# Two of three attention units by rows until unit 121, and LayerNorm statistics a slot earlier

## The chip, the cores and the metric

The kernel runs on one NeuronCore of a Trainium2 chip. Its engines are TensorE (PE, with its weight loads shown as PEld), VectorE (DVE), ScalarE (ACT), GpSimd (POOL) and SyncE (SP), which issues nearly all DMAs. Each engine works through its own queue in order and waits on semaphores of the others. The metric is the device time of one execution in microseconds, as the median of several runs.

## The reference

One block of a conditioned transformer: an attention with cached keys and values, then a gated MLP with a spatial mixing matrix, each behind a LayerNorm that is modulated by a condition vector `c`.

```python
mod = (_silu(c) @ w_mod).reshape(c.shape[0], 6, 1, -1)      # sa, ca, ga, sb, cb, gb
h = _layernorm(x) * (1 + ca) + sa
# A: q = h @ wq (32 heads of 128), 8 groups of cached k, v; softmax(q k / sqrt(128)) v @ wo
x = x + ga * _A_ref(h, A_k_cache, A_v_cache, A_wq, A_wo)
h = _layernorm(x) * (1 + cb) + sb
# B: z = gelu(h @ w_in); z1, z2 = halves; z2 = _layernorm(z2); g = w_sp @ z2 + b_sp; (z1 * g) @ w_out
x = x + gb * _B_ref(h, B_w_in, B_w_sp, B_b_sp, B_w_out)
```

There are 2048 tokens of 512 features in bfloat16, 2048 cached keys, 8 groups of 4 heads that share keys and values, and 896 features in each half of the MLP.

## The kernel before

**Units and passes.** Attention is cut into 128 units: 8 groups times 16 tiles of 128 tokens. Unit u belongs to group u // 16 and tile j = u % 16, and covers the 4 heads of its group. The main loop has one pass `it` for each unit and six more at its end; pass `it` makes the scores of unit `it`, the PV sum (probabilities times values) of earlier units, and the output projection of still earlier ones. A pass has 8 slots. The order inside a slot is fixed by the program: first what `at(it, slot, fn)` has put down for it (the list `later`, in the order of registration), then the scores `qk`, then PV, then a piece of the next block's q projection (`fill`), then a matmul of the output projection, which takes the last slots of a pass. The schedule is manual, so each engine's queue keeps the program's order.

**Two forms of a unit.** A *column unit* computes the scores transposed (L1029), keys on the partitions; ScalarE's exponential writes them straight into `pTs[u]`. PV then takes 64 matmuls of 129 columns (`pv`, L1085), the last column being the row sum; DVE divides (L1096, L1097: `onorm`), SP turns the result by a DMA transpose into `oT` (L1108), and the output projection sums 4 matmuls in one PSUM bank, which DVE adds to `xacc` once (L1129). A *row unit* computes the scores with queries on the partitions (L1010); the exponential (L1017) writes rows into one of six row buffers `pn` and leaves sums, SP transposes each head's rows into `pTs[u]` (`turn_rows`, L1049), and DVE makes the reciprocal of the sums (L1053, L1056). PV takes 16 matmuls of 512 columns (`pv_rows`, L1064) and DVE copies them to `oT` (L1073). Each head's projection matmul then has a bank of its own, which DVE scales and adds to `xacc` (L1135, four times). The `pn` buffers lie where `win_sb`, the MLP's first weight, is loaded later (L1276).

`by_rows(u)` says which form a unit has: from TURN_A = 8 up to TURN_B, two of every three. `LAGS` gives a row unit's PV two or three passes after its scores; a column unit's comes one pass after.

```python
TURN_A, TURN_B = 2 * CT, NU - CT * 2 - 1     # 8 and 119; NU = 128, CT = 4
LAGS = (2, 3, 1)
def by_rows(u):
    return TURN_A <= u < TURN_B and (u - TURN_A) % len(LAGS) < len(LAGS) - 1
def pv_at(u):
    return u + (LAGS[(u - TURN_A) % len(LAGS)] if by_rows(u) else 1)
def wo_at(u):
    return pv_at(u) + (3 if u < NU - 6 else 2)
```

With this, passes 118, 119, 120, 121, 122, 123 hold the PV of units 116, 118, 117 and 119, 120, 121, 122, and passes 121 to 126 hold the output projections of 116; 118; 117 and 119; 120; 121 and 122; 123.

**Banks.** PSUM has two banks of scores (`s_ps`, each 1024 wide), two `o_ps` banks for PV and two `misc` banks, which the q projection (L946, cast to SBUF by DVE at L957) and the output projection (L1142) take in turn.

**The end of a tile.** When the last group's projection of tile j is complete, `xacc` times `ga_rows` plus x becomes the new `x_sb` tile: on POOL for tiles 0 to 11 (L1158, L1159), on DVE for 12 to 15. `ln2` then normalises it in three steps, put down for later slots: `first` takes the statistics on DVE (L697 bn_stats, L698) and the reciprocal root on POOL (L678, L682); `second` normalises on DVE (L686) and has SP transpose the result into `xnT2` (L1180; two buffers); `third` modulates it into the MLP's input `hT` on DVE (L1187, four instructions).

Of the kernel before, what the change touches and what calls it, by code (L numbers as in the profile page):

```python
# [575 lines left out]
def kernel(  # L576
# [28 lines left out]
    NT = S // P  # L605
# [4 lines left out]
    CT = 512 // P  # L610
# [64 lines left out]
    def rstd_of(mv, n, tag):  # L675

        ve = stat.tile([P, CT], FP32, name=f"ve_{tag}")
        nc.gpsimd.tensor_scalar(  # L678
            out=ve[:, :n], in0=mv[:, :, 1], scalar1=LN_EPS, scalar2=None, op0=ALU.add
        )  # L680
        rstd = stat.tile([P, CT], FP32, name=f"rstd_{tag}")
        nc.gpsimd.tensor_tensor(out=rstd[:, :n], in0=ve[:, :n], in1=mhalf[:, :n], op=ALU.pow)  # L682
        return rstd

    def normalise(dst, src, mv, rstd):
        nc.vector.tensor_scalar(  # L686
            out=dst,
            in0=src,
            scalar1=mv,
            scalar2=rstd,  # L690
            op0=ALU.subtract,
            op1=ALU.mult,
        )

    def ln_stats(mv, j, src):
        st = stat.tile([P, 1, nc.vector.BN_STATS_DIM], FP32, name="bnst")
        nc.vector.bn_stats(out=st[:, 0, :], in_=src)  # L697
        nc.vector.bn_aggr(out=mv[:, j, :], in_=st[:])  # L698
# [97 lines left out]
    def ln1_stats(j0, n):  # L796
        for j in range(j0, j0 + n):
            ln_stats(mv1, j, x_sb[:, j, :])
        return rstd_of(mv1[:, j0 : j0 + n, :], n, "ln1")
# [161 lines left out]
    first = dict(r1=ln1_stats(1, 1))  # L961


    NU = HKV * NT


    TURN_A, TURN_B = 2 * CT, NU - CT * 2 - 1

    LAGS = (2, 3, 1)

# [21 lines left out]
    def at(it, slot, fn):  # L992
        later.setdefault((it, slot), []).append(fn)
# [173 lines left out]
    def ln2(it, j):  # L1167

        st = {}

        def first():
            if j < NT - CT:
                ln_stats(mv2, j, x_sb[:, j, :])
            st["rstd"] = rstd_of(mv2[:, j : j + 1, :], 1, "ln2")

        def second():
            xn = res.tile([P, D], BF16, name="xn2", bufs=2)
            normalise(xn[:], x_sb[:, j, :], mv2[:, j, 0:1], st["rstd"][:, 0:1])
            st["xnT"] = res.tile([P, NDT, P], BF16, name="xnT2", bufs=2)
            nc.sync.dma_start_transpose(out=st["xnT"][:], in_=xn[:])  # L1180

        def third():
            ch, c0 = j // CT, (j % CT) * P
            if ch not in h2Ts:
                h2Ts[ch] = res.tile([P, NDT, 512], BF16, name="hT", bufs=NCH)
            for dt in range(NDT):
                nc.vector.tensor_scalar(  # L1187
                    out=h2Ts[ch][:, dt, c0 : c0 + P],
                    in0=st["xnT"][:, dt, :],
                    scalar1=modc[:, 4 * NDT + dt : 4 * NDT + dt + 1],  # L1190
                    scalar2=modc[:, 3 * NDT + dt : 3 * NDT + dt + 1],
                    op0=ALU.mult,
                    op1=ALU.add,
                )

        at(it + 1, 0 if j >= NT - CT else 3, first)
        at(it + 1, 4 if j >= NT - CT else 5, second)
        at(it + 2, 5, third)

    mod_b = {}  # L1200
# [109 lines left out]
    for g in range(1, HKV):  # L1310
        it = (g - 1) * NT
# [106 lines left out]
    for it in range(NU + 6):  # L1418
# [26 lines left out]
        for u in wos:  # L1445
            if u >= (HKV - 1) * NT:
                ln2(it, u % NT)
# [185 lines left out]
```

## Time and profile before

| | |
|---|---|
| median of 3 runs | 1308.66 us (1308.49 to 1308.84) |
| the profiled execution | 1308.74 us |
| its span, first to last instruction | 1306.8 us |
| PE busy | 1298.8 us, 99% of the span |
| ACT busy | 1113.5 us, 85% |
| DVE busy | 674.7 us, 52% |
| POOL busy | 56.6 us, 4% |
| granted TensorE clock | 1.000 |

The profile is of one execution. Busy is the time in which an engine ran at least one instruction; a matmul's end is modelled and matmuls overlap, so the spacing of starts tells more than durations. A timeline line has the start, the duration of what is merged in it, the engine, the source line and the operation with what it writes and reads; in square brackets stands how long the engine was idle before it, and what ended that. A wait line has who waited, for whom, the total, how often and the longest.

### The profile page before, as it was taken

The numbers are of one execution on the slowest core, as the hardware profiler recorded it, in microseconds if no ns is written. First come the engines' busy times: TensorE is split into PE (matmuls) and PEld (weight loads), VectorE is DVE, ScalarE is ACT, GpSimd is POOL, SyncE is SP. The second block draws the span as 40 slices with busy tenths as digits, with TensorE's granted clock in tenths as the row PEclk, the third lists the DMA queues.
The fourth block names the chain that finished last, engine by engine and source line by source line (L and its number), as shares of the span: only waits on it lengthen the run. The fifth ranks groups of instructions, "written<-read, shape, count | busy, mean of one in ns | idle before, by whom it ended". The sixth has DMA issues, their size and how long they took to land.

```text
span 1306.8 us, 22904 instructions
## 1 busy us (share of the span) xinstructions
PE 1298.8 (99%) x8809; PEld 705.7 (54%) x8809; DVE 674.7 (52%) x1740; ACT 1113.5 (85%) x1653; POOL 56.6 (4%) x92
## 2 busy tenths in 40 slices
PE   9999999999999999999999999999999999999998
PEld 5665555555555555555555555555555566644445
DVE  5534445544554455445544554455455657694443
ACT  7899999999999999999999999999999988650000
POOL 1000000000000000000000000000000134210000
PEclk9999999999999999999999999999999999999999
DMA  7469999999999999999999999999999921364300
GB/s 183 125 127 188 163 193 183 190 168 187 189 188 168 192 168 195 177 170 186 189 189 170 187 189 179 180 188 174 182 187 171 166 82 29 57 137 98 78 20 31
DMA packets 743878, 203.33 MB, mean 156 GB/s; under 512 B 728144, under 2 KB 742608, under 8 KB 743760
## 3 DMA queue, kind: packets, MB, share of 16 engines
q1 hardware_dynamic: 741168, 199.55, 83.1%
q10 hardware_dynamic: 2592, 2.23, 0.6%
q8 instruction: 71, 1.16, 0.4%
q14 instruction: 47, 0.39, 0.1%
HBM read 21.37 MB, written 2.10 MB: 18 GB/s over the span
## 4 chain that ended last, share of the span: by engine, by line
PE 92%; DVE 0%; issue 0%
PE o_ps L1064 20%; PE s_ps L1010 19%; PE o_ps L1085 13%; PE s_ps L1029 12%; PE misc L1142 8%; PE misc L946 8%; PE misc L1500 7%; PE s_ps L1335 2%; PE s_ps L1374 2%; PE o_ps L1533 1%; PE s_ps L1533 0%; PE o_ps L856 0%; DVE xacc L1135 0%; DVE tmp L1545 0%; DVE bnst L697 0%; DVE qT L957 0%
## 5 line engine op out<-in xcount | busy, mean ns | idle before, releaser
L1010 PE MATMUL s_ps<-kT,qT 128*128 128x512 bf16 x1184 | 352.1, 379 | 0.2 <-ACT pn L1017 0.2
L1017 ACT ACTIVATE win_sb<-s_ps 128x1024 bf16<-128x1024 f32 x298 | 305.1, 1024 | 3.1 <-ACT win_sb L1017 0.5
L1036 ACT ACTIVATE pT<-s_ps 128x1024 bf16<-128x1024 f32 x256 | 258.8, 1026 | 16.8 <-PE s_ps L1029 4.8
L1064 PE MATMUL o_ps<-pT,v 128*128 128x512 bf16 x896 | 265.8, 379 | 0.0
L1029 PE MATMUL s_ps<-qT,kT 128*128 128x512 bf16 x864 | 256.8, 379 | 0.3 <-ACT pT L1036 0.2
L1135 DVE SCALAR_TENSOR_TENSOR xacc<-misc,rall,xacc 128x512 f32<-128x512 f32 x290 | 217.1, 749 | 55.5 <-PE misc L1142 49.3
L1017 ACT ACTIVATE pn<-s_ps 128x1024 bf16<-128x1024 f32 x196 | 200.7, 1025 | 1.2
L1142 PE MATMUL misc<-wo_g,oT 128*128 128x512 bf16 x512 | 194.0, 379 | 0.6 <-DVE qT L957 0.6
L1064 PEld LDWEIGHTS <-v 128*128 128x128 bf16 x1184 | 115.8, 98 | 139.7
L1036 ACT ACTIVATE wsp<-s_ps 128x1024 bf16<-128x1024 f32 x176 | 179.5, 1024 | 13.4 <-PE s_ps L1029 5.6
L946 PE MATMUL misc<-hT,wq_g 128*128 128x512 bf16 (+2 forms) x528 | 190.7, 371 | 0.1
L1010 PEld LDWEIGHTS <-qT 128*128 128x128 bf16 x1184 | 115.5, 98 | 103.9 <-issue 0.7
L1085 PEld LDWEIGHTS <-pT 128*128 128x128 bf16 x2048 | 136.8, 98 | 59.0
L957 DVE CAST qT<-misc 128x512 bf16<-128x512 f32 x127 | 87.2, 687 | 156.5 <-PE misc L946 156.4
L1085 PE MATMUL o_ps<-v,pT 128*128 128x129 bf16 x2048 | 157.2, 220 | 0.0
L1053 DVE TENSOR_TENSOR tot<-rs 128x1 f32<-128x1 f32 x296 | 46.3, 157 | 165.4 <-ACT win_sb L1017 110.1
L1029 PEld LDWEIGHTS <-kT 128*128 128x128 bf16 x864 | 83.6, 98 | 86.6 <-issue 1.8
L1085 PEld LDWEIGHTS <-wsp 128*128 128x128 bf16 x1408 | 94.3, 98 | 41.5
L1085 PE MATMUL o_ps<-v,wsp 128*128 128x129 bf16 x1408 | 108.5, 220 | 0.0
L1017 ACT ACTIVATE wmod_a<-s_ps 128x1024 bf16<-128x1024 f32 x98 | 100.3, 1024 | 0.3 <-ACT wmod_a L1017 0.3
L1500 PE MATMUL misc<-wsp,z 128*128 128x512 bf16 (+2 forms) x560 | 100.5, 336 | 0.0
L1064 PE MATMUL o_ps<-wsp,v 128*128 128x512 bf16 x288 | 85.7, 379 | 0.0
(107 smaller groups left out, 861.0 us busy)
## 6 DMA issues: line engine op xcount, KB each, us to landing
wo_g<-in_A_wo_dram SPq DMA_DIRECT2D x8, 512.0 KB, 4.7
wq_g<-in_A_wq_dram SPq DMA_DIRECT2D x7, 512.0 KB, 4.4
v<-in_A_v_cache_dram SPq DMA_DIRECT2D x7, 512.0 KB, 4.8
wsp<-in_w_mod_dram SPq DMA_DIRECT2D x1, 2048.0 KB, 8.8
out_dram<-yout ACTq DMA_DIRECT2D x16, 128.0 KB, 1.7
pT<-win_sb SPq DMA_TRANSPOSE x113, 4.8
win_sb<-in_B_w_in_dram SPq DMA_DIRECT2D x1, 1792.0 KB, 7.4
x_sb<-in_A_x_dram SPq DMA_DIRECT2D x3, 512.0 KB, 5.6
```

Of the source, the lines that this page charges most:

```text
L946: nc.tensor.matmul(ps[0][:, o0 : o0 + n], lhsT=wqs[g][:, dt, hh * DH : (hh + 1) * DH], rhs=hTs[ch][:, dt, c0 : c0 + n], start=(dt == 0), s ...
L957: nc.vector.tensor_copy(out=dst, in_=src)
L1010: nc.tensor.matmul(s_ps[:, c * 512 : (c + 1) * 512], lhsT=qTs[b][:, hh, jj * P : (jj + 1) * P], rhs=groups[g]["kT"][:, k0 : k0 + 512], sta ...
L1017: nc.scalar.activation(out=rows_of(u, hh)[:, half * HK : (half + 1) * HK], in_=s_ps[:], func=ACT.Exp, scale=inv_sqrt_dh, accum_out=rsums[u ...
L1029: nc.tensor.matmul(s_ps[:, h * 512 : (h + 1) * 512].rearrange("p (r q) -> p r q", r=REP), lhsT=groups[g]["kT"][:, kt * P : (kt + 1) * P], ...
L1036: nc.scalar.activation(out=pTs[u][:, 2 * i : 2 * i + 2, :], in_=s_ps[:].rearrange("p (k q) -> p k q", k=2), func=ACT.Exp, scale=inv_sqrt_dh,)
L1053: nc.vector.tensor_tensor(out=tot[:], in0=rs[:, 2 * hh : 2 * hh + 1], in1=rs[:, 2 * hh + 1 : 2 * hh + 2], op=ALU.add)
L1064: nc.tensor.matmul(o_pss[u][:], lhsT=groups[g]["v1"][:, kt, 0:DH], rhs=pTs[u][:, kt, :], start=(kt == 0), stop=(kt == NKT - 1),)
L1085: nc.tensor.matmul(o_ps[:, hh % 2, 0 : DH + 1], lhsT=pTs[u][:, kt, hh * P : (hh + 1) * P], rhs=groups[g]["v1"][:, kt, 0 : DH + 1], start=( ...
L1135: nc.vector.scalar_tensor_tensor(out=xa[:], in0=X_ps[:], scalar=scale, in1=xa[:], op0=ALU.mult, op1=ALU.add)
L1142: nc.tensor.matmul(ps[0][:], lhsT=oTs[u][:, hh, :], rhs=groups[g]["wo"][:, hh, :], start=(hh == 0 or each), stop=(hh == REP - 1 or each),)
L1500: nc.tensor.matmul(g_pss[f][:, :n], lhsT=z2[:, st, f * P : (f + 1) * P], rhs=wsp[t][:, st, c0 : c0 + n], start=(st == 0), stop=(st == NT - ...
```

## The change

TURN_B becomes 122, so units 119 and 120 are row units too; 118 and 121 are column units as before. Their PV passes become 121 and 123, and unit 121's stays 122, so that pass 120 holds the PV of 117 alone and pass 123 that of 120 and 122. Their output projections move to passes 124 and 126, beside unit 123's in the latter. The oT transpose of unit 118, whose PV pass is now a row unit's, is issued at the start of the next pass. The load of `win_sb` moves from pass 120 to pass 123. For tiles 0 to 11, `first` moves from slot 3 to slot 2 of the pass after the projection, and `second` from slot 5 to slot 4; `third` stays.

```diff
-    TURN_A, TURN_B = 2 * CT, NU - CT * 2 - 1
+    TURN_A, TURN_B = 2 * CT, NU - 6
 ...
-        at(it + 1, 0 if j >= NT - CT else 3, first)
-        at(it + 1, 4 if j >= NT - CT else 5, second)
+        at(it + 1, 0 if j >= NT - CT else 2, first)
+        at(it + 1, 4, second)
         at(it + 2, 5, third)
```

## The prediction

> **What bounds the kernel now.** I read the page first: the span, the busy shares, and then the list of what TensorE waited for.
>
> ```profile
> span 1306.8 us, 22904 instructions
> ...
> PE 1298.8 (99%) x8809; PEld 705.7 (54%) x8809; DVE 674.7 (52%) x1740; ACT 1113.5 (85%) x1653; POOL 56.6 (4%) x92
> ```
>
> ```profile
> PE o_ps L787 <- DVE onorm L768: 1.2, 1, 1.2
> PE misc L1142 <- DVE qT L957: 0.6, 1, 0.6
> ...
> PE s_ps L1010 <- ACT pn L1017: 0.2, 1, 0.2
> ```
>
> TensorE (PE) is busy for 99% of the span, and its waits are a handful. It waits once for the warm-up's zeros, once for 0.6 us at the output projection (L1142), and 0.2 us for an exponential (L1010 is the score matmul of a row unit, so ScalarE keeps up with row units at no price worth a term). So the change can gain only by cheaper matmuls and by taking that L1142 wait away, and it can lose only by making PE wait somewhere new.
>
> The second view is the PE timeline of the last group: start, duration, instruction. Durations overlap, so I use differences of starts. "Pass n" is the pass of the main loop in which the scores of unit n are made.
>
> ```profile
> 1017.00 0.59 PE L1010 MATMUL s_ps<-kT,qT 128*128 128x512 bf16 x2
> ...
> 1034.44 0.59 PE L1029 MATMUL s_ps<-qT,kT 128*128 128x512 bf16 x2
> ...
> 1035.52 0.59 PE L1029 MATMUL s_ps<-qT,kT 128*128 128x512 bf16 x2
> ...
> 1043.07 0.59 PE L1029 MATMUL s_ps<-qT,kT 128*128 128x512 bf16 x2
> ...
> 1051.88 0.59 PE L1029 MATMUL s_ps<-qT,kT 128*128 128x512 bf16 x2
> ...
> 1064.14 0.59 PE L1029 MATMUL s_ps<-qT,kT 128*128 128x512 bf16 x2
> ...
> 1074.05 0.59 PE L1029 MATMUL s_ps<-qT,kT 128*128 128x512 bf16 x2
> ...
> 1074.93 0.38 PE L946 MATMUL misc<-hT,wq_g 128*128 128x512 bf16 x1
> 1075.15 0.59 PE L1029 MATMUL s_ps<-qT,kT 128*128 128x512 bf16 x2
> ...
> 1081.75 0.59 PE L1029 MATMUL s_ps<-qT,kT 128*128 128x512 bf16 x2
> ...
> 1088.80 0.38 PE L1142 MATMUL misc<-wo_g,oT 128*128 128x512 bf16 x1 [0.57 <-DVE qT L957]
> ...
> 1092.32 0.59 PE L1029 MATMUL s_ps<-qT,kT 128*128 128x512 bf16 x2
> ...
> 1100.10 0.38 PE L1142 MATMUL misc<-wo_g,oT 128*128 128x512 bf16 x1
> ...
> 1109.12 0.59 PE L1029 MATMUL s_ps<-qT,kT 128*128 128x512 bf16 x2
> ```
>
> Passes 116, 118, 119, 120, 121, 123, 124 and 126 start at 1017.00, 1034.44, 1043.07, 1051.88, 1064.14, 1081.75, 1092.32 and 1109.12. A slot with two score matmuls, a row unit's PV and one more matmul takes 1035.52 - 1034.44 = 1.08 us: five matmuls of 512 columns at 0.216. With a column unit's PV it takes 1075.15 - 1074.05 = 1.10, of which the last matmul starts 0.88 in. Eight slots make a pass of 8.64 or 8.80.
>
> **The change, part by part.** *Two PV sums by rows.* Units 119 and 120 become row units. Their score matmuls and their four output projection matmuls stay as many as they were; the PV falls from 1.10 to 1.08 per slot, so 16 x 0.02 = **-0.32 us**. [...]
>
> *The double pass moves.* Unit 117 has a lag of 3, so pass 120 now holds the PV of both 117 and 119 (12.26 us long). Afterwards the double pass is 123 (PV of 120 and 122): the same work three passes later, free in itself. But pass 123 today has two output projections (117 and 119) beside a q projection. Its work is eight slots of 1.10 and four more matmuls of 0.216, 9.66 us; it lasted 1092.32 - 1081.75 = 10.57. The 0.91 lost includes the 0.57 of the L1142 row: each row-unit matmul takes a `misc` bank of its own, one of the two banks holds the q projection, and VectorE (DVE) is late. Afterwards 119 projects in pass 124 and 120 in pass 126, where no q projection runs. The loss goes: **-0.91**.
>
> *What becomes late instead.* Two row-unit projections take on new neighbours, and the statistics (`first`) and normalisation (`second`) of tiles 0 to 11 move ahead in DVE's in-order queue. This is the DVE timeline of pass 121, and GpSimd's (POOL's) last step there.
>
> ```profile
> 1031.12 0.15 DVE L1053 TENSOR_TENSOR tot<-rs 128x1 f32<-128x1 f32 x1
> ...
> 1031.40 0.75 DVE L1135 SCALAR_TENSOR_TENSOR xacc<-misc,rall,xacc 128x512 f32<-128x512 f32 x1
> ...
> 1064.67 0.74 DVE L1135 SCALAR_TENSOR_TENSOR xacc<-misc,rall,xacc 128x512 f32<-128x512 f32 x1
> 1068.03 0.70 DVE L697 BATCH_NORM_STATS2 bnst<-x_sb 128x6 f32<-128x512 bf16 x1 [2.62 <-POOL x_sb L1159]
> ...
> 1068.86 0.14 DVE L1096 RECIPROCAL rall<-o_ps 128x2 f32<-128x2 f32 x1
> ...
> 1069.37 0.68 DVE L957 CAST qT<-misc 128x512 bf16<-128x512 f32 x1
> 1069.97 0.74 DVE L1135 SCALAR_TENSOR_TENSOR xacc<-misc,rall,xacc 128x512 f32<-128x512 f32 x1
> 1070.63 0.97 DVE L1187 TENSOR_SCALAR hT<-xnT,modc 128x128 bf16<-128x128 bf16 x4
> 1071.52 0.41 DVE L686 TENSOR_SCALAR xn<-x_sb,mv,rstd_ln 128x512 bf16<-128x512 bf16 x1
> 1071.84 1.60 DVE L1135 SCALAR_TENSOR_TENSOR xacc<-misc,rall,xacc 128x512 f32<-128x512 f32 x2
> ...
> 1113.82 0.69 DVE L697 BATCH_NORM_STATS2 bnst<-x_sb 128x6 f32<-128x512 bf16 x1 [1.80 <-POOL x_sb L1159]
> ```
>
> ```profile
> 1065.49 1.27 POOL L1158 TENSOR_TENSOR xacc<-xacc,ga_rows 128x512 f32<-128x512 f32 x1 [7.92 <-DVE xacc L1135]
> ...
> 1069.34 0.57 POOL L682 TENSOR_TENSOR rstd_ln<-ve_ln,mhalf 128x1 f32<-128x1 f32 x1
> ```
>
> The last projection of the pass before ends at 1064.67 + 0.74 = 1065.41; POOL then makes x_sb, and bn_stats (L697) starts at 1068.03, 2.62 later and X = 3.89 into the pass. POOL, not the slot number, sets that time, so moving `first` a slot earlier buys nothing; it only puts a longer wait ahead of what DVE has queued. Steps from X, by starts: 0.83 to the next work, 0.51 for a column unit's L1096 and L1097 (1068.86 to 1069.37), 0.60 for the q cast, 0.66 for a projection's L1135, 0.89 for `third` (L1187 x4), 0.32 for L686; L1053 and L1056, two per row unit's head, 0.28 (1031.12 to 1031.40). POOL's reciprocal root ends at 1069.91 = X + 1.88.
>
> Today the order is cast, L1135 of projection 0, `third`, L686, L1135 of projection 1. With `second` at slot 4, L686 comes first and must wait for POOL, to X + 1.91; behind it stand the projections' L1135, for whose banks PE waits. So L1135 of projection 0 ends at X + 1.91 + 0.32 + 0.75 = X + 2.98, and that of projection 1, after 0.66 - 0.75 + 0.89 + 0.75 more, at X + 4.53 (4.81 where scores are by rows). PE needs the latter's bank for projection 3, which is due in slot 7: 7 x 1.08 + 0.86 = 8.42 into a row-PV pass. Adding 0.08 for the signal, as POOL starts 1065.49 - 1065.41 after DVE ends:
> - Pass 120 (projects 114): 3.89 + 4.81 + 0.08 = 8.78 against 8.42, **+0.36**.
> - Pass 121 (projects 116): DVE ends pass 120 late. From L1135 of projection 1 (starts 7.95) come 0.66, 0.28, 0.66 and the oT cast at 0.60, so the last L1135 runs 10.15 to 10.90 and X is 13.52, or 4.52 into pass 121 (which starts 8.64 + 0.36 later). 4.52 + 4.53 + 0.08 = 9.13 against 8.42, **+0.71**.
> - Pass 124 (projects 119): X 3.89, so 8.50; due at 1100.10 - 1092.32 = 7.78, **+0.72**.
> - Pass 126 (projects 120 in slots 0 to 3, 123 after): `first` of tile 10 stands at slot 2, ahead of projection 2's L1135, which is out of the bank at X + 0.83 + 0.75 + 0.08. The bank is due at 4 x 1.10 + 0.88 = 5.28. X is 3.89 as elsewhere, or 1113.82 - 1109.12 = 4.70 as pass 126 has it now: 0.27 to 1.08. Only one tile's `third` (not two, as now) precedes the add in pass 125, so I take a value near the low end, **+0.40**.
>
> Pass 117 has no `third` and passes 119, 122 and 125 project column units, which hold one bank: 0. In pass 123 slots last 1.5 us: 0.
>
> *Transposes.* Each new row unit adds four 128 x 2048 DMA transposes to SP's queue.
>
> ```profile
> 1019.87 7.54 SPq L1049 DMA_TRANSPOSE pT<-win_sb  x3
> 1027.51 3.44 SPq L1049 DMA_TRANSPOSE pT<-wmod_a  x1
> ...
> 1049.43 1.49 SPq L1180 DMA_TRANSPOSE xnT<-xn  x1
> ...
> ```
>
> ```profile
> DMA to landing us min/median/max: 4.2/4.7/7.2
> ```
>
> ```profile
> win_sb<-in_B_w_in_dram SPq DMA_DIRECT2D x1, 1792.0 KB, 7.4
> ```
>
> Unit 116 issued its first 1019.87 - 1017.00 = 2.87 into its pass, three in 7.54 (2.51 each). For 119 the first goes at 1045.94, but the second now stands behind `second`'s transpose of tile 1, which waits for DVE (1049.43 today; 0.28 later with L1053 queued behind `first`). It leaves SP free at about 1051.2, so the fourth issues at 1056.2 and lands at 1060.4, 1060.9 or 1063.4 by the three landing times. The PV of 119 begins 0.43 into pass 121, at 1051.88 + 8.64 + 0.36 + 0.43 = 1061.31. Median: covered by 0.4 us, **0**; a longer wait would first swallow pass 121's 0.71. For unit 120 (lag 3) there is a pass to spare. The w_in load goes from pass 120 to 123 and takes 7.4 us; it is used from pass 128, over two passes past 1109.12: 0. In pass 126 a third xnT2 tile is alive for two buffers, so SP waits one slot for `third` of tile 7; behind it is only an oT transpose used two passes on: 0, and one slot if that cover went.
>
> Sum: the profiled execution took 1308.74 us, its span of 1306.8 and 1.9 around it; the median of the runs is 0.08 less. 1308.74 - 0.32 - 0.91 + 0.36 + 0.71 + 0.72 + 0.40 = 1309.70, so 1309.6 as a median. That is 0.07% up, within the 0.2% (2.6 us) that a measurement of this kernel can tell from no change.
>
> **Rivals.** *DVE keeps up.* Each new wait is 0.4 to 0.7 us; if L686 is not held by POOL, or the banks rotate more kindly, none shows: 1308.66 - 1.23 = 1307.4. For it: today's order fits in every pass but 123. Against it: X is set by POOL, in row after row.
>
> *Unit 119's transposes come late* (slower). Place: the start of pass 121, where PV needs all four heads. The fourth at 1027.51 took 3.44 on SP; with three such and the longest landing, 7.2, it lands at 1051.2 + 6.9 + 7.2 = 1065.3, PE stands for 4.0 in place of 0.71: 1312.9. It decides from a landing at 1063.7 (a wait of 2.4) on, where the total passes 1311.3. For it: SP is idle for xn while heads are ready. Against it: the median row leaves 0.4 spare. [...]
>
> *PV by rows saves more* than the spacing of starts shows: faster. To pass 1306.0 with no new wait at all, each of the two units would have to save 0.16 + 1.4 / 2 = 0.9 us, five times what the rows of 1.08 and 1.10 give, so I leave it little. [...]
>
> *The statistics do not move at all*, since POOL sets X: part of the forecast, not apart from it.
>
> **How the numbers follow.** Forecast 0.58, of which 0.04 beyond 1311.3 if pass 126 takes its upper end and the others slip by 0.3 each; DVE keeps up 0.20; late transposes 0.18; rows much cheaper, or an unknown gain, 0.04. So faster 0.04, same 0.54 + 0.20 = 0.74, slower 0.22. The range goes from the first rival's 1307.4 to 1311.6, a little into the second's.
>
> **What would show it.** Pass 123's L1142 row with the 0.57 wait on the q cast is gone; new PE waits at L1142 on DVE appear in passes 120, 121, 124 and 126, each under 1.1 us; bn_stats still starts 3.8 to 4.6 into its pass; L686 follows POOL's L682 directly. A PE wait of L1064 on a transpose at the start of pass 121 would show the second rival; PE waits that sum to under 1 us the first. Wrong altogether: a wait in the passes from 128 on, or slots other than 1.08 and 1.10.

## The result, and the profile after

The changed kernel takes 1310.09 us (median of 22 runs, 1309.63 to 1310.76), the kernel before 1308.63 (22 runs on the same chip, 1308.23 to 1309.16): 1.46 us more, a ratio of 1.0012 with a 95% interval of 1.0006 to 1.0017. The forecast was 1309.6, +0.96 on the profile's own time. Its profiled execution took 1310.3 us. The page begins:

```profile
span 1308.4 us, 22621 instructions
...
PE 1290.1 (99%) x8557; PEld 701.4 (54%) x8713; DVE 678.8 (52%) x1756; ACT 1115.2 (85%) x1669; POOL 56.3 (4%) x92
```

The trace lacks 156 matmul records (8713 weight loads, 8557 matmuls), so PE's 1290.1 us of busy time is not to be compared with the 1298.8 of before.

TensorE's waits, from the list of waits of the changed kernel (us in total, times, longest):

```profile
PE o_ps L787 <- DVE onorm L768: 1.2, 1, 1.2
PE misc L1142 <- DVE xacc L1135: 1.1, 3, 0.5
```

The row of before, L1142 on the q cast, is gone. In its place L1142 waits three times for an L1135. Where, the PE timeline of the changed kernel shows: the starts of passes 120 to 127, and the L1142 rows at which something is lost.

```profile
1051.84 0.59 PE L1010 MATMUL s_ps<-kT,qT 128*128 128x512 bf16 x2
...
1060.52 0.38 PE L1142 MATMUL misc<-wo_g,oT 128*128 128x512 bf16 x1
1060.73 0.59 PE L1029 MATMUL s_ps<-qT,kT 128*128 128x512 bf16 x2
...
1069.83 0.38 PE L1142 MATMUL misc<-wo_g,oT 128*128 128x512 bf16 x1 [0.31 <-DVE xacc L1135]
1070.05 0.59 PE L1029 MATMUL s_ps<-qT,kT 128*128 128x512 bf16 x2
...
1078.85 0.59 PE L1029 MATMUL s_ps<-qT,kT 128*128 128x512 bf16 x2
...
1091.11 0.59 PE L1029 MATMUL s_ps<-qT,kT 128*128 128x512 bf16 x2
...
1099.59 0.38 PE L1142 MATMUL misc<-wo_g,oT 128*128 128x512 bf16 x1 [0.29 <-DVE xacc L1135]
1099.81 0.59 PE L1029 MATMUL s_ps<-qT,kT 128*128 128x512 bf16 x2
...
1108.61 0.59 PE L1029 MATMUL s_ps<-qT,kT 128*128 128x512 bf16 x2
...
1114.59 0.38 PE L1142 MATMUL misc<-wo_g,oT 128*128 128x512 bf16 x1 [0.53 <-DVE xacc L1135]
...
1118.11 0.59 PE L1029 MATMUL s_ps<-qT,kT 128*128 128x512 bf16 x2
```

The passes last 8.89, 9.32, 8.80, 12.26, 8.70, 8.80 and 9.50 us. The bracket shows less than is lost, since it counts from a modelled end; differences of starts show all of it. L1142 at 1060.52 has no bracket, yet it starts 8.68 into its pass where 8.42 was due.

Now the DVE timeline of passes 120, 121 and 124, and POOL's last step in pass 120:

```profile
1055.67 0.69 DVE L697 BATCH_NORM_STATS2 bnst<-x_sb 128x6 f32<-128x512 bf16 x1 [2.35 <-POOL x_sb L1159]
...
1057.58 0.41 DVE L686 TENSOR_SCALAR xn<-x_sb,mv,rstd_ln 128x512 bf16<-128x512 bf16 x1 [0.17 <-POOL rstd_ln L682]
...
1058.18 0.73 DVE L1135 SCALAR_TENSOR_TENSOR xacc<-misc,rall,xacc 128x512 f32<-128x512 f32 x1
1058.83 0.98 DVE L1187 TENSOR_SCALAR hT<-xnT,modc 128x128 bf16<-128x128 bf16 x4
1059.71 0.75 DVE L1135 SCALAR_TENSOR_TENSOR xacc<-misc,rall,xacc 128x512 f32<-128x512 f32 x1
...
1065.25 0.69 DVE L697 BATCH_NORM_STATS2 bnst<-x_sb 128x6 f32<-128x512 bf16 x1 [2.35 <-POOL x_sb L1159]
...
1067.16 0.41 DVE L686 TENSOR_SCALAR xn<-x_sb,mv,rstd_ln 128x512 bf16<-128x512 bf16 x1 [0.42 <-POOL rstd_ln L682]
...
1095.00 0.69 DVE L697 BATCH_NORM_STATS2 bnst<-x_sb 128x6 f32<-128x512 bf16 x1 [2.61 <-POOL x_sb L1159]
...
1096.91 0.41 DVE L686 TENSOR_SCALAR xn<-x_sb,mv,rstd_ln 128x512 bf16<-128x512 bf16 x1 [0.49 <-POOL rstd_ln L682]
```

```profile
1056.98 0.57 POOL L682 TENSOR_TENSOR rstd_ln<-ve_ln,mhalf 128x1 f32<-128x1 f32 x1
```

Pass 120 reads from top to bottom as forecast: bn_stats (L697) starts X = 3.83 into the pass, POOL's L682 runs until 1057.55, and behind it come L686, L1135 of projection 0, `third`, L1135 of projection 1 until 1060.46, and PE's L1142 of projection 3 at 1060.52. L686 is held by L682 in passes 121 and 124 as well.

The span grew by 1.58 us. Passes 120 to 126 sum to 66.27 us, against 65.24 before: +1.03. Pass 120 starts 0.03 earlier, and from the start of pass 127 to the last weight load (L1533) both kernels take 184.14. The remaining 0.58 lies behind the last weight load, where the prediction had no term.

### The profile page after: what moved, and what is told of

It is laid out like the page before. It is cut to its first block, busy times and chain, and to the rows that moved or that the text cites. A ratio compares the mean times of both kernels' runs of the same rounds, so it can differ in the third digit from the quotient of the medians.

```text
span 1308.4 us, 22621 instructions
## 1 busy us (share of the span) xinstructions
PE 1290.1 (99%) x8557; PEld 701.4 (54%) x8713; DVE 678.8 (52%) x1756; ACT 1115.2 (85%) x1669; POOL 56.3 (4%) x92
## 4 chain that ended last, share of the span: by engine, by line
PE 89%; DVE 2%; POOL 1%; issue 1%; DVEq 0%
PE s_ps L1010 20%; PE o_ps L1064 19%; PE o_ps L1085 12%; PE s_ps L1029 11%; PE misc L1142 7%; PE misc L1500 7%; PE misc L946 7%; PE s_ps L1335 2%; PE s_ps L1374 2%; PE o_ps L1533 1%; DVE xacc L1135 1%; POOL xacc L1158 0%; POOL x_sb L1159 0%; PE s_ps L1533 0%; DVE hT L1187 0%
## 5 line engine op out<-in xcount | busy, mean ns | idle before, releaser
L1010 PE MATMUL s_ps<-kT,qT 128*128 128x512 bf16 x1192 | 356.5, 379 | 2.6 <-ACT pn L1017 0.2
L1017 ACT ACTIVATE win_sb<-s_ps 128x1024 bf16<-128x1024 f32 x306 | 313.3, 1024 | 3.1 <-ACT win_sb L1017 0.5
L1135 DVE SCALAR_TENSOR_TENSOR xacc<-misc,rall,xacc 128x512 f32<-128x512 f32 x298 | 222.9, 748 | 54.0 <-PE misc L1142 47.7
L1029 PE MATMUL s_ps<-qT,kT 128*128 128x512 bf16 x832 | 247.2, 379 | 1.4 <-ACT pT L1036 0.2
L1017 ACT ACTIVATE pn<-s_ps 128x1024 bf16<-128x1024 f32 x200 | 204.8, 1025 | 1.2
L1142 PE MATMUL misc<-wo_g,oT 128*128 128x512 bf16 x478 | 181.1, 379 | 2.2 <-DVE xacc L1135 1.1
L946 PE MATMUL misc<-hT,wq_g 128*128 128x512 bf16 (+2 forms) x491 | 177.2, 370 | 0.6
L1036 ACT ACTIVATE wsp<-s_ps 128x1024 bf16<-128x1024 f32 x160 | 163.6, 1024 | 8.2 <-PE s_ps L1029 0.5
L1085 PEld LDWEIGHTS <-wsp 128*128 128x128 bf16 x1280 | 85.7, 98 | 37.8
L1085 PE MATMUL o_ps<-v,wsp 128*128 128x129 bf16 x1280 | 98.7, 220 | 0.4
```

What stands on the lines that cost most here:

```text
L946: nc.tensor.matmul(ps[0][:, o0 : o0 + n], lhsT=wqs[g][:, dt, hh * DH : (hh + 1) * DH], rhs=hTs[ch][:, dt, c0 : c0 + n], start=(dt == 0), s ...
L1010: nc.tensor.matmul(s_ps[:, c * 512 : (c + 1) * 512], lhsT=qTs[b][:, hh, jj * P : (jj + 1) * P], rhs=groups[g]["kT"][:, k0 : k0 + 512], sta ...
L1017: nc.scalar.activation(out=rows_of(u, hh)[:, half * HK : (half + 1) * HK], in_=s_ps[:], func=ACT.Exp, scale=inv_sqrt_dh, accum_out=rsums[u ...
L1029: nc.tensor.matmul(s_ps[:, h * 512 : (h + 1) * 512].rearrange("p (r q) -> p r q", r=REP), lhsT=groups[g]["kT"][:, kt * P : (kt + 1) * P], ...
L1036: nc.scalar.activation(out=pTs[u][:, 2 * i : 2 * i + 2, :], in_=s_ps[:].rearrange("p (k q) -> p k q", k=2), func=ACT.Exp, scale=inv_sqrt_dh,)
L1085: nc.tensor.matmul(o_ps[:, hh % 2, 0 : DH + 1], lhsT=pTs[u][:, kt, hh * P : (hh + 1) * P], rhs=groups[g]["v1"][:, kt, 0 : DH + 1], start=( ...
```

## The experiments

All passes below are differences between first weight loads in the trace, in us. Each median stands beside that of the kernel before on the same chip.

| kernel | 120 | 121 | 122 | 123 | 124 | 125 | 126 | sum | median | before | ratio, 95% |
|---|---|---|---|---|---|---|---|---|---|---|---|
| before | 12.26 | 8.81 | 8.81 | 10.56 | 8.00 | 8.81 | 8.00 | 65.24 | | | |
| changed | 8.89 | 9.32 | 8.80 | 12.26 | 8.69 | 8.80 | 9.50 | 66.27 | 1310.09 | 1308.63 | 1.0012, 1.0006 to 1.0017 |
| rows only | 8.63 | 8.65 | 8.80 | 12.26 | 8.11 | 8.80 | 8.81 | 64.07 | 1307.64 | 1308.47 | 0.9994, 0.9985 to 1.0003 |
| slots only | 12.26 | 8.81 | 8.81 | 10.08 | 8.00 | 8.81 | 8.00 | 64.76 | 1308.30 | 1308.47 | 0.9999, 0.9990 to 1.0008 |
| rows, `first` at 2 | 8.63 | 8.79 | 8.80 | 12.26 | 8.11 | 8.80 | 9.50 | 64.90 | 1308.61 | 1308.47 | 1.0001, 0.9992 to 1.0010 |
| rows, `second` at 4 | 8.97 | 9.32 | 8.80 | 12.26 | 8.70 | 8.80 | 8.81 | 65.67 | 1309.33 | 1308.47 | 1.0007, 0.9998 to 1.0016 |
| changed, again | 8.88 | 9.31 | 8.80 | 12.26 | 8.68 | 8.80 | 9.49 | 66.23 | 1309.91 | 1308.38 | 1.0012, 1.0003 to 1.0021 |
| changed, x_sb on DVE | 8.63 | 8.63 | 8.81 | 12.26 | 8.00 | 8.81 | 8.97 | 64.11 | 1307.85 | 1308.38 | 0.9995, 0.9986 to 1.0004 |
| rows, x_sb on DVE | 8.63 | 8.63 | 8.81 | 12.26 | 8.00 | 8.81 | 8.81 | 63.94 | 1307.57 | 1308.38 | 0.9995, 0.9986 to 1.0004 |
| changed, `second` at 3 | 9.47 | 9.91 | 8.80 | 12.26 | 9.22 | 8.80 | 10.60 | 69.07 | 1313.17 | 1308.38 | 1.0036, 1.0023 to 1.0050 |

### The two halves, and the two slots

Rows only, the slots as before:

```diff
-    TURN_A, TURN_B = 2 * CT, NU - CT * 2 - 1
+    TURN_A, TURN_B = 2 * CT, NU - 6
```

> TURN_B is 122 as in the changed kernel; first and second stay at slots 3 and 5. Theory (DVE's order): the new PE waits of the changed kernel come from first and second standing earlier in DVE's queue. The lost time of pass 123 (0.91 us) and the PV's 0.32 are gained; the chain of pass 120 ends at X + 4.33 = 8.30 in place of 8.70 and fits, pass 121 is late by about 0.1, pass 124 by 0.15, pass 126 not at all. Time 1308.63 - 1.23 + 0.25 = 1307.6. Rival (load): two more row units simply load DVE and SP more, wherever the statistics stand; then this kernel is as slow as the changed one, 1310.1.

Slots only, the rows as before:

```diff
-        at(it + 1, 0 if j >= NT - CT else 3, first)
-        at(it + 1, 4 if j >= NT - CT else 5, second)
+        at(it + 1, 0 if j >= NT - CT else 2, first)
+        at(it + 1, 4, second)
```

> TURN_B stays 119; first and second move to slots 2 and 4. Theory (DVE's order): no new wait, since before pass 122 no row unit projects in a pass that has both second and third ahead of it except pass 121, where column PV gives slots of 1.10 us and the chain just fits; in pass 123 the statistics of tile 6 go ahead of the third projection and the lost 0.91 falls to about 0.4. Time 1308.63 - 0.5 = 1308.1. Rival (slots cost by themselves): the moves bring waits of the size of the changed kernel's, 1309.5 or more.

The rows with `first` alone moved (slot 2, `second` at 5), and with `second` alone moved (slot 4, `first` at 3):

> TURN_B 122, first at slot 2, second still at slot 5. Theory: in passes 120, 121 and 124 the projections' L1135 no longer stand behind L686 and POOL, so these waits fall to about 0.16, 0.23 and 0.15; pass 126 keeps the changed kernel's 0.70, since there it is the statistics of tile 10 that stand ahead of projection 2. Time 1308.63 - 1.3 + 1.24 = 1308.6. Rival (load): 1310.1.

> TURN_B 122, first still at slot 3, second at slot 4. Theory: passes 120, 121 and 124 keep the changed kernel's waits (0.26, 0.69, 0.70), pass 126 has none, since projection 2's L1135 now stands ahead of the statistics. Time 1308.63 - 1.3 + 1.65 = 1309.0. Rival (load): 1310.1.

The rows alone come out 0.83 us under the kernel before, the slots alone 0.17 (their passes 0.48, all of it in pass 123). So neither half is slower; the loss is made where they meet. The table shares it out: `second` at slot 4 alone makes the waits of passes 120, 121 and 124 (+0.34, +0.67 and +0.59 over rows only), `first` at slot 2 alone that of pass 126 (+0.69) and 0.14 of pass 121. One line of the list of waits carries it in each: `first` alone, then `second` alone.

```profile
PE misc L1142 <- DVE xacc L1135: 0.5, 1, 0.5
```

```profile
PE misc L1142 <- DVE xacc L1135: 0.8, 3, 0.3
```

With rows only no L1142 row stands in that list at all. By the intervals none of these four kernels can be told from the kernel before; the passes tell them apart. Their sum repeats to 0.04 us between two profiles of the changed kernel. Pass by pass these four came within 0.16 us of what was expected, the medians within 0.33.

### Is it POOL that holds the chain?

If X and L682 make the waits, taking POOL out of x_sb must remove them, with the change left whole:

```diff
-            engine = nc.gpsimd if j < NT - CT else nc.vector
+            engine = nc.gpsimd if 8 <= j < NT - CT else nc.vector
```

> The changed kernel with x_sb of tiles 0 to 7 made on DVE in place of POOL, so the statistics of these tiles need not wait 2.5 us for POOL; tiles 8 to 11 stay on POOL. Theory (POOL's lateness, met in order by DVE): X falls from 3.9 to about 2.7 in passes 118 to 125, the reciprocal root is there before slot 4, and the waits of passes 120, 121 and 124 vanish (8.63, 8.63, 8.0), although DVE has 1.4 us more to do in each; pass 126 (tiles 9 and 10) keeps 9.50. Time about 1308.5 - 1.3 + 0.7 = 1307.9. Rival (DVE's own load is the bound): more work on DVE makes the projections later still, above 1310.1.

The same edit on rows only:

> TURN_B 122, first and second at slots 3 and 5, and x_sb of tiles 0 to 7 on DVE. Theory: the 0.13 us that rows alone still loses in passes 121 and 124 goes, so 1307.5, the same as rows alone within what the median tells. Rival (DVE's load): worse than rows alone by 0.5 or more.

The waits of passes 120, 121 and 124 go to zero in both. The DVE timeline of pass 120 of the first of the two, which starts at 1051.89 there, shows how: no bracket names POOL.

```profile
1054.74 0.68 DVE L697 BATCH_NORM_STATS2 bnst<-x_sb 128x6 f32<-128x512 bf16 x1
...
1057.02 0.40 DVE L686 TENSOR_SCALAR xn<-x_sb,mv,rstd_ln 128x512 bf16<-128x512 bf16 x1
```

bn_stats starts 2.85 into the pass in place of 3.83, and L686 runs 2.28 after it, behind the cast, when L682 has ended (at 1056.60). Pass 126 loses 0.16, where 0.70 was expected; its tile is one that POOL still adds, and the part on pass 126 below comes back to it. With rows only, what was left (0.02, 0.11) goes too, and 63.94 is the sum with none of these waits: the gain of the rows is 1.30.

### The other way: `second` a slot earlier still

```diff
-        at(it + 1, 4, second)
+        at(it + 1, 4 if j >= NT - CT else 3, second)
```

> The changed kernel with second at slot 3 for tiles 0 to 11, one slot earlier still. Theory: L686 cannot run before X + 1.9 in any case, but now also the q cast and the column units' L1096 and L1097 stand behind it. Pass 120 loses about 0.9 in place of 0.26, pass 121 1.3 in place of 0.69, pass 124 1.2 in place of 0.69, pass 126 keeps 0.70: 1308.5 - 1.3 + 4.1 = 1311.3. Rival (load): the slot does not matter, 1310.1; rival (an earlier slot makes the tile ready earlier and helps): under 1310.

The direction is right and the size is not: 1313.17 against 1311.3. Passes 120, 121 and 124 lose 0.84, 1.28 and 1.22 us, near the 0.9, 1.3 and 1.2 expected. The miss lies in pass 126, which loses 1.79 in place of 0.70 (PE waits there for an L1129 too), and in pass 117 (9.19 in place of 8.63), which was not expected: L686 now stands ahead of the q cast as well, so the bank of the q projection is held too. The waits, and DVE in pass 117:

```profile
PE misc L1142 <- DVE qT L957: 1.8, 3, 1.1
PE misc L1142 <- DVE xacc L1135: 1.6, 3, 0.7
PE misc L1142 <- DVE xacc L1129: 0.8, 1, 0.8
```

```profile
1031.58 0.41 DVE L686 TENSOR_SCALAR xn<-x_sb,mv,rstd_ln 128x512 bf16<-128x512 bf16 x1 [0.77 <-POOL rstd_ln L682]
1031.91 0.68 DVE L957 CAST qT<-misc 128x512 bf16<-128x512 f32 x1
```

DVE stands 0.77 us for L682, and the cast behind it ends at 1032.59; the next L1142 starts at 1032.64. Going from slot 4 to 3 costs 2.80 us in passes 120 to 126 and 0.56 in pass 117; from 5 to 4 it cost 1.37 (66.27 against 64.90).

### The missing half microsecond

The changed kernel once more, to see whether its excess is that of the passes:

> The changed kernel once more, on the chip of the next three. Of its 1.46 us over the kernel before, the passes account for 1.0; the other 0.5 lies behind the last matmul. Theory (passes alone): those 0.5 are the variation of single executions (from the last L1533 weight load to the end of the span the six profiles so far take 5.7 to 6.4 us), so the median comes out 1.0 to 1.2 above the kernel before, and the passes are the same to 0.1. Rival (a longer ending): the ending of this kernel is 0.5 longer each time, so 1.5 again with an ending of 6.3 or more.

1.53 us over the kernel before, with an ending (last weight load to the end of the span) of 6.38: the theory fell and the rival stood. Every kernel with TURN_B = 122 so far had it: from the landing of the last output DMA to the end 2.37 us, against 1.86 and 1.79 with TURN_B = 119. SyncE's records in the trace show what runs there: eight waits, one for each semaphore of its DMAs (L1598), then eight more (L1628), of 0.06 to 0.10 us each, and a handshake of all engines. In the kernel before the last output DMA uses the third semaphore, in the changed one the first, so that 16 waits come after the landing in place of 14; and one step takes 0.38 us in place of 0.07. The row change brings eight transposes of pT and takes away two of oT. So the theory was that the turn of the semaphores sets the longer ending. Two splits of the `win_sb` load on rows only, into three DMAs and into eight, and one on the kernel before, into seven, change the number of DMAs and leave the passes alone:

```diff
-    at(TURN_B + 1, 2, lambda: nc.sync.dma_start(out=win_sb, in_=win_dram))
+    for f0, f1 in zip([0, 600, 1192], [600, 1192, 1792]):
+        at(TURN_B + 1, 2, lambda f0=f0, f1=f1: nc.sync.dma_start(
+            out=win_sb[:, :, f0:f1], in_=win_dram[:, :, f0:f1]))
```

> The kernel with rows until unit 121 and tile statistics at slots 3 and 5, with the load of the input projection's weights (L1276) issued as three DMAs in place of one: two DMAs more, nothing else. Theory, the ending is set by which of the eight queue semaphores the last output DMA uses, so by the number of DMAs before it: the last landing to the end of the span 1.86 us in place of 2.37 (up to 2.2 if a 0.38 us step between two waits of SyncE stays), the ending 5.7 to 5.8 us, the time 1307.2 us, at most 1307.5. Rival, the longer ending belongs to the row form and not to the number of DMAs: 2.37 us again, the time 1307.6 us. Both: passes 120 to 126 sum to 64.07 us as without the split.

> The same kernel with that load issued as eight DMAs: seven DMAs more. Theory, as before: the turn of the semaphores goes on by seven, so that the last output DMA's semaphore is waited for last of the eight, seven waits of about 0.08 us are passed before the landing, and from the last landing to the end of the span it takes about 1.8 us (1.5 if the 0.38 us step goes too); the time 1307.0 to 1307.1 us. Rival, the ending belongs to the row form: 2.37 us and 1307.6 us. Both: passes 120 to 126 sum to 64.07 us.

> The kernel before, with that load issued as seven DMAs in place of one: six DMAs more, the number by which the row form exceeds it, no unit by rows. Theory: the last landing to the end of the span rises from 1.86 us to 2.37, the ending from 5.8 to 6.2 to 6.4 us, the time from 1308.5 to 1309.0 us, with passes 120 to 126 at 65.24 us as before. Rival, the ending belongs to the row form: 1.86 us and 1308.5 us.

| kernel | SyncE instructions | waits after the landing | the 0.38 us step | landing to end | median | before |
|---|---|---|---|---|---|---|
| before | 869 | 14 | none | 1.86 | | |
| changed, and seven others with rows | 880 | 16 | at the 14th wait | 2.37 | | |
| rows only, load in 3 | 882 | 14 | at the 12th of 16 | 2.17 | 1307.48 | 1308.44 |
| rows only, load in 8 | 887 | 9 | none after the landing | 2.00 | 1307.17 | 1308.44 |
| before, load in 7 | 875 | 16 | in the handshake | 1.96 | 1308.71 | 1308.44 |
| rows, x_sb on DVE, load in 17 | 896 | 16 | none | 1.96 | 1307.36 | 1308.59 |

The semaphores turned as the theory said: first, third or eighth by the number of DMAs. The price did not. Sixteen waits after the landing cost the kernel before only 0.10 us more in its profile, where 0.5 was expected, and its excess of 0.27 us is inside an interval of 0.9992 to 1.0010. With the load in eight, only nine waits are left, but SyncE then stands 0.61 us for ScalarE's own closing wait, which sets 2.00 in place of the 1.8 expected. The passes kept their sums: 64.06, 64.07 and, for the kernel before, 65.23.

What the larger part of the longer ending goes by stands in the fourth column. Counted from the program's start, the 0.38 us step comes at SyncE's 873rd recorded instruction in every kernel that shows it: the 860th is the first closing wait with 880 instructions (873 is the 14th), the 862nd with 882 (the 12th), the 855th with 875 (the 19th, in the handshake, where other engines' work hides most of it). The kernel before ends at its 869th and never comes to it. That gave the last test, on rows only with x_sb on DVE: sixteen DMAs more, two full turns of the eight semaphores, so that the count moves and the last semaphore does not.

```diff
+    win_cut = [0] + [112 * k for k in range(1, 16)] + [1736, 1792]
+    for k in range(17):
+        at(TURN_B + (1 if k < 12 else 3), 2 if k < 12 else 5,
+           lambda f0=win_cut[k], f1=win_cut[k + 1]: nc.sync.dma_start(
+               out=win_sb[:, :, f0:f1], in_=win_dram[:, :, f0:f1]))
```

> Rows until unit 121, the slots of before, x_sb of tiles 0 to 7 on VectorE, and the load of the input projection's weights issued as 17 DMAs in place of one: sixteen more, two full turns of the eight queue semaphores, so that the last output DMA uses the same semaphore as without them and all eight waits come after its landing. Theory, the 0.38 us step stands at the 873rd instruction of SyncE, wherever that falls: it now falls before the first of the closing waits (the 875th or 876th instruction), under the last landing, and the last landing to the end of the span takes 1.99 us in place of 2.37; the time 1307.57 - 0.38 = 1307.2 us. Rival, the step belongs to the row form with that semaphore: 2.37 us and 1307.6 us. Both: passes 120 to 126 sum to 63.94 us.

1.96 us and no step, with all sixteen waits after the landing and passes of 63.95. The median is 1.23 us below the kernel before on its chip, where the same kernel without the split was 0.81 below: 0.42 gained, which is less than the intervals can tell but agrees with the profiles' 0.41 (2.37 to 1.96). So of the 0.51 by which the changed kernel's ending is longer after the landing, 0.41 goes with the step and 0.10 with the two waits more. With 17 DMAs the 873rd instruction stands ahead of the closing waits and comes 0.53 us after the 872nd, as far as the same two instructions lie apart in the kernel before: no step can be told there, and whether it is hidden or absent is not shown. Why the step comes at that instruction is open.

The best of all these, rows only with the load in eight, has a ratio of 0.9990, 0.9981 to 0.9999: 1.27 us or 0.1% faster, with an interval that only just leaves out no change.

## Why the prediction came out

**The PV by rows and pass 123's lost time.** Forecast -0.32 and -0.91, together -1.23. Measured -1.30, as the sum of the passes with every wait removed, 63.94 against 65.24. Right as a sum; no run takes the two apart. That the row of before would go, and that its price would go with it, holds.

**Pass 120.** Forecast +0.36, measured +0.26. X came at 3.83 in place of 3.89, the chain behind it took 4.79 in place of 4.81, and the signal, from DVE's end to PE's start, 0.06 in place of 0.08.

**Pass 121.** Forecast X at 4.52 and +0.71. L697 starts at 1065.25, 4.52 into the pass, and projection 3 at 1069.83, 9.10 in where 8.42 was due: +0.68.

**Pass 124.** Forecast X at 3.89 and +0.72. L697 starts at 1095.00, 3.89 into the pass, projection 3 at 1099.59, 8.48 in where 7.78 was due: +0.70.

**Pass 126.** Forecast +0.40 out of 0.27 to 1.08, measured +0.70: this term of the sum was mis-sized, and the step that was off is X. I put it near 4.0, since one tile's `third` and not two comes before the add in pass 125. The DVE and POOL timelines of the changed kernel there:

```profile
1106.46 2.78 DVE L1187 TENSOR_SCALAR hT<-xnT,modc 128x128 bf16<-128x128 bf16 x4
...
1109.69 0.68 DVE L1129 TENSOR_TENSOR xacc<-misc,xacc 128x512 f32<-128x512 f32 x1
...
1112.99 0.69 DVE L697 BATCH_NORM_STATS2 bnst<-x_sb 128x6 f32<-128x512 bf16 x1 [0.30 <-POOL x_sb L1159]
...
1113.82 0.72 DVE L1135 SCALAR_TENSOR_TENSOR xacc<-misc,rall,xacc 128x512 f32<-128x512 f32 x1
```

```profile
1106.30 1.37 POOL L1158 TENSOR_TENSOR xacc<-xacc,ga_rows 128x512 f32<-128x512 f32 x1 [0.23 <-DVE xacc L1129]
1107.75 1.21 POOL L1159 TENSOR_TENSOR x_sb<-xacc,x_sb 128x512 bf16<-128x512 f32 x1
...
1110.45 1.28 POOL L1158 TENSOR_TENSOR xacc<-xacc,ga_rows 128x512 f32<-128x512 f32 x1 [1.49 <-DVE xacc L1129]
1111.80 1.16 POOL L1159 TENSOR_TENSOR x_sb<-xacc,x_sb 128x512 bf16<-128x512 f32 x1
```

There is one `third` (L1187 x4), as forecast, but it takes 2.78 us, not 0.98 as in pass 120, and POOL is at work on another tile from 1106.30 to 1108.96. L1129 ends at 1110.37, POOL's add follows it, and L697 of tile 10 starts 4.38 into the pass. From there the forecast's steps hold: L1135 of projection 2 starts 0.83 later, and PE's L1142 at 1114.59. That POOL's work is what stretches L1187 is read from these rows and from the whole trace: 58 instructions of L1187 without POOL beside them have a median of 0.31 us, the three covered by it at least four fifths 1.22, and each of the three ends 0.05 us after POOL's L1158 or L1159. No run took that work away, and why the one stretches the other is not shown.

The stretch alone does not make the wait. With x_sb of tiles 0 to 7 on DVE, `third` of pass 125 is as long, and yet tile 10's L697 comes at 3.89:

```profile
1104.07 2.78 DVE L1187 TENSOR_SCALAR hT<-xnT,modc 128x128 bf16<-128x128 bf16 x4
1107.01 0.17 DVE L1096 RECIPROCAL rall<-o_ps 128x2 f32<-128x2 f32 x1 [0.16 <-PE o_ps L1085]
...
1110.92 0.66 DVE L697 BATCH_NORM_STATS2 bnst<-x_sb 128x6 f32<-128x512 bf16 x1
```

There `third` starts 5.85 into pass 125 in place of 6.65, because tile 7's bn_stats, ahead of it on DVE, starts at 2.83 in place of 4.39; DVE is free again in time for PE, and pass 126 loses only 0.16. So most of the 0.70 hangs on the late start, and that on POOL's x_sb of tile 7. That it also takes the long `third` is an estimate: with 0.98 us in place of 2.78 it would have ended at 1107.44, ahead of the 8.79 us into the pass (1108.60) at which PE lets L1096 go in the run just shown. The forecast had neither the late start nor the long `third`.

**Transposes.** Forecast: unit 119's fourth lands at 1060.9 and is covered by 0.4 us.

```profile
1051.10 1.92 SPq L1049 DMA_TRANSPOSE pT<-wmod_a  x1
1053.12 4.90 SPq L1049 DMA_TRANSPOSE pT<-pn  x2
```

```profile
DMA to landing us min/median/max: 4.7/4.8/4.9
```

```profile
1061.16 0.59 PE L1064 MATMUL o_ps<-pT,v 128*128 128x512 bf16 x2
```

The first of the four goes ahead of tile 1's transpose (at 1045.91, as forecast) and three behind it, the fourth lands at 1060.47, and the first PV matmul of pass 121 starts at 1061.16 with no bracket: 0.7 to spare. With rows only, where pass 121 starts earlier, the landing comes at 1059.20 and the PV at 1060.76, again without a wait. The second rival was not met in any run. The first, that DVE keeps up, is refuted by the waits of four passes, and is what happens once POOL is taken out of x_sb.

**The sum.** Waits of 0.26, 0.68, 0.70 and 0.70 are 2.34 against 2.19 forecast, gains 1.30 against 1.23: +1.03 of passes against +0.96. The passes come out within 0.1 us of the forecast, in part by luck: the errors of the four waits (-0.10, -0.03, -0.02, +0.30) and of the gain (-0.07) partly cancel. The forecast of 1309.6 fell 0.5 short of the median for a reason of its own: it took everything behind pass 127 as constant. "Each new row unit adds four transposes to SP's queue" was followed to their landings and not to SyncE's closing instructions, where it costs 0.51 of the ending's 0.58; the other 0.07 is a later landing (4.02 after the last weight load, against 3.95).

**Signs named beforehand.** L1142 waits in passes 120, 121, 124 and 126, each under 1.1 us; bn_stats at 3.83, 4.52, 3.89 and 4.38 ahead of them, inside 3.8 to 4.6 (the first of two in pass 126, tile 9's, came at 3.19, outside it); L686 directly behind L682 in passes 120, 121 and 124; no wait from pass 128 on: met but for that.

## What to carry to other kernels

An instruction moved earlier on an in-order engine is not free when its input comes from another engine: find the hand-over that sets the input's time (here X and POOL's L682), and if that does not move, everything between the old slot and the new one now waits for it (with `second` at slot 4, PE lost 0.34, 0.67 and 0.59 us by it in passes 120, 121 and 124). Two edits that are each harmless can be slower together (here 0.83 and 0.17 us under the kernel before apart, 1.46 over it together), so the slots want measuring with the rows and not apart. And sum the whole span: a microsecond's worth of argument in the passes can be shifted by half of one in the closing waits (here 0.51 us beside the 1.03 of the passes).

## What was not expected of the hardware

SyncE takes a step of 0.38 us at its 873rd recorded instruction in every kernel here in which that is one of its instructions after the last landing (875, 880 and 882 in all). Eleven more instructions on its queue brought the changed kernel to it, and 0.41 of its 1.46 us went with it. Its cause is not shown.

DVE's `third` took 2.78 us beside POOL's adds of 512 columns and 0.98 without. Beside POOL's L682, which has one column, an L1187 kept its 0.30 to 0.31 us (the kernel before, from 1097.51 on).
